# A float64 weight conversion in four planned stages, and stores of transformed rows issued from ScalarE's queue

## The chip, the cores and the metric

The kernel runs on one core of one Trainium2 chip. The metric is the device time of one execution in microseconds (us). The core has a matrix engine (TensorE, PE in the profile; its weight loads are PEld), a vector engine (VectorE, DVE), a scalar engine (ScalarE, ACT), a general engine (GpSimd, POOL) and an engine that here only issues DMA transfers (SyncE, SP). Each engine works through its own instructions in order. SP, ACT and POOL can issue transfers; "SPq" and "ACTq" in the profile are their issuing queues, and a transfer that has to wait there holds back whatever the same engine issues or computes behind it.

## The reference

```python
def reference(x, w_r, w_i, b_r, b_i, moe_w_in, moe_w_out, moe2_w_gate, moe2_w1, moe2_w2, moe2_capacity):
    X = np.fft.rfft(x, axis=1)                       # x: 8 x 3072 x 256
    Yr = X.real @ w_r - X.imag @ w_i + b_r
    Yi = X.real @ w_i + X.imag @ w_r + b_i
    Yr, Yi = (np.sign(v) * np.maximum(np.abs(v) - 0.01, 0) for v in (Yr, Yi))
    y = np.fft.irfft(Yr + 1j * Yi, n=3072, axis=1).astype(np.float32)
    x = y.reshape(8 * 3072, 256)
    h = x @ moe_w_in                                 # float64 weights, 256 x 2048
    g = np.where(h > 0, h, np.exp(np.minimum(h, 0)) - 1)
    x = (g @ moe_w_out).astype(np.float32)           # float64 weights, 2048 x 256
    # top-1 routing to 8 experts with a capacity: gate, pack, two matmuls
    # (256 -> 1024 -> 256, relu between), scaled by the gate and put back
    return moe2(x, moe2_w_gate, moe2_w1, moe2_w2, moe2_capacity)
```

## The kernel before

**The stages.** The 3072-point transforms are done in two steps of 96 and 32 points as matmuls. The first transform has steps s1 (line 144, its result `zo` stored to DRAM as `zs`) and s2 (line 174, reads `zi` back); then comes the spectral product `mix` (L219 to L237; `k` is a copy of one matmul's result, L221, which the matmul of L224 waits for); then the inverse transform with i1 (L249, result copied to `vo` and stored as `vs` by ACT, L253 and L254) and i2 (L273, reads `vi` back from `vs`, ACT copies the result to `yt`, L274, and SP stores it as `ys`, L276). The rows in `ys` are the tokens of the feed-forward part: `load_y` (L434) reads them as `y`, `split_y` (L442, L443) splits them into two parts `x`, `up` (L456 to L464) and `down` (L478) are its two matmuls. The experts follow (L582 and on). Only the first 14 chunks of 512 tokens, from a little over two batches, are worked out unconditionally; that is all that this profile holds.

**The float64 weights.** `moe_w_in` and `moe_w_out` come as float64. They are converted in 16 pieces of 128 by 512 numbers, 8 of each (`f64_piece`, L410; `f64_parts`, L376 to L397), into two float32 parts that are kept in SBUF: `win` and `wout`. A piece is a load `fv` of 512 KB by SP, a Square on ACT (`fsq`, L388), six VectorE instructions (L389, L390, L391, L393, L395, L396), a cast on ACT (L392, the first part) and two POOL instructions (L394, L397, the second part). All of its tiles, `fv`, `fsq`, `fh`, `fa` and `fb`, have a single buffer, so that a piece can only be loaded once the one before has been read.

**What sets the order.** The front of the program, up to the first matmuls of the feed-forward part, is a `plan`: a list of (time, piece of work), sorted by time and run by `run_until(t)`. One unit of time is one step `u` of `smi_pieces` (s2, and mix a little later); a batch has `nu` = 12 of them. The 16 weight pieces are spread over the times 1 to 28 with the whole piece at one time. A scheduler then orders each engine's instructions, with the plan's order as its priority, except that transfers issued through `load` (L114) keep the program's order on SP. The constants of the routing part (`wg`, `id`, `fv`<-`cst`, `e`, `tok`, and the cast of L821 that reads that `fv`) are loaded between `run_until(2 * nu + 3)` and `run_until(2 * nu + 6)`, thus ahead of the last weight piece.

Of the kernel before, what the change touches and what calls it, by code (L numbers as in the profile page):

```python
# [13 lines left out]
I32 = mybir.dt.int32  # L14
AF = mybir.ActivationFunctionType
ALU = mybir.AluOpType
# [15 lines left out]
MIX_LAG, I1_LAG = 2.2, 4.15  # L32
S1_AHEAD, X_AHEAD = 3, 2
S1_END, I2_END = 4, 4
W_SPAN = 1, 28
W_EARLY = 4
FF_START, FF_STEP = -1.8, 0.5

# [78 lines left out]
def f32(ap):  # L117
    return ap.bitcast(F32)


class Fft:
# [142 lines left out]
    def i2(self, i, ys, m=NA):  # L264
        nc = self.nc
        v = self.vt.pop(i)
        g, dh, h = i // 4, i // 2 % 2, i % 2
        if h == 0:
            self.yt = self.p["y"].tile([128, NA, 8], F32, name="yt")
        ps = self.bank("i2", [128, 512])  # L270
        pv = ps[:, 0:4 * m].rearrange("p (j n) -> p j n", j=4)
        for j in range(4):
            nc.tensor.matmul(pv[:, j, :], v[:, j, :], self.k["f2"][:, 0:m])  # L273
        nc.scalar.copy(self.yt[:, 0:m, 4 * h:4 * h + 4].rearrange("p n j -> p j n"), pv)  # L274
        if h == 1:
            nc.sync.dma_start(ys[dh, :, g, 0:m, :], self.yt[:, 0:m, :])  # L276


def fft_consts(tc, pool, tmp, cst, w_r, w_i, b_r, b_i):
# [95 lines left out]
def f64_parts(tc, tmp, src, p1, p2):  # L375

    nc, n = tc.nc, int(np.prod(src.shape[1:]))
    v = tmp.tile([128, 2 * n], I32, name="fv").rearrange("p (n t) -> p n t", t=2)
    sv = src.bitcast(I32)
    load(tc, v, sv.rearrange("p (n t) -> p n t", t=2) if len(sv.shape) == 2  # L380
                      else sv.rearrange("p a (n t) -> p a n t", t=2))
    hi, lo = v[:, :, 1], v[:, :, 0]
    sq = tmp.tile([128, n], F32, name="fsq")
    h = tmp.tile([128, n], I32, name="fh")
    a = tmp.tile([128, n], I32, name="fa")
    b = tmp.tile([128, n], I32, name="fb")
    least = float(np.array([0x380C0000], np.uint32).view(np.float32)[0])
    nc.scalar.activation(sq, f32(hi), AF.Square)  # L388
    nc.vector.scalar_tensor_tensor(f32(h), sq, least * least, f32(hi), op0=ALU.is_ge, op1=ALU.mult)  # L389
    nc.vector.tensor_scalar(a, h, 3, 0x3FFFFFF8, op0=ALU.logical_shift_left, op1=ALU.bitwise_and)  # L390
    nc.vector.scalar_tensor_tensor(b, h, -0x40000000, a, op0=ALU.bitwise_and, op1=ALU.bitwise_or)  # L391
    nc.scalar.copy(p1, f32(b))  # L392
    nc.vector.tensor_scalar(a, b, -0x00800000, None, op0=ALU.bitwise_and)  # L393
    nc.gpsimd.tensor_tensor(f32(b), f32(b), f32(p1), op=ALU.subtract)  # L394
    nc.vector.tensor_scalar(h, lo, 1, None, op0=ALU.logical_shift_right)  # L395
    nc.vector.scalar_tensor_tensor(sq, h, 2.0 ** -51, f32(a), op0=ALU.mult, op1=ALU.mult)  # L396
    nc.gpsimd.tensor_tensor(p2, f32(b), sq, op=ALU.add)  # L397


def scatter(tc, group, dst, idx, src, rows, free=True):  # L400
# [8 lines left out]
def f64_piece(tc, tmp, w_in, w_out, win, wout, i):  # L409

    if i < 8:
        a, c = divmod(i, 4)
        sl = slice(c * 512, c * 512 + 512)
        f64_parts(tc, tmp, w_in[a * 128:a * 128 + 128, sl], *(w[:, a, sl] for w in win))
    else:
        fs = slice(2 * (i - 8), 2 * (i - 8) + 2)
        f64_parts(tc, tmp, w_out.rearrange("(f p) d -> p f d", p=128)[:, fs, :],
                  *(w[i - 8].rearrange("p f d -> p (f d)") for w in wout))


# [281 lines left out]
def kernel(ctx, tc, x, w_r, w_i, b_r, b_i, moe_w_in, moe_w_out, w_gate, w1, w2, cst, out, cap):  # L702
    nc = tc.nc
# [13 lines left out]
    ys = [dr1.tile([2, 128, 4, NA, 8], F32, name=f"ys{b}") for b in range(3)]  # L717
# [7 lines left out]
    win = [wpool.tile([128, 2, DFF], F32R, name=f"win{i}") for i in (1, 2)]  # L725
    wout = [[], []]
# [19 lines left out]
    fp.update({n: mk(s1st, "f_" + n, b, side="right") for n, b in dict(x=3, z=2).items()})  # L746
    fp0["z"] = Cycle(fp["z"], mk(x0st, "f_z0", 2))

    def w_piece(i):
        f64_piece(tc, fp["f64"], moe_w_in, moe_w_out, win, wout, i)  # L750

    k, kfirst = fft_consts(tc, fp["c"], fp["sh"], cst, w_r, w_i, b_r, b_i)
    tags = dict(s1=["pd"], s2=["pb", "pc"], mix=["pa"], i1=["pd"], i2=["pd"])
# [20 lines left out]
    def i2p(b, m=NA):  # L774
        return [lambda i=i: i2(b, i, m) for i in range(-1, 16)]
# [4 lines left out]
    def at(t0, t1, pieces):  # L780
        plan.extend((t0 + (t1 - t0) * (n + 0.5) / len(pieces), len(plan) + n, f) for n, f in enumerate(pieces))

    def run_until(t):
        plan.sort(key=lambda v: v[:2])
        while plan and plan[0][0] < t:
            plan.pop(0)[2]()
# [19 lines left out]
    at(0.5, nu - S1_END, s1p(1)[S1_AHEAD:])  # L806
    at(nu - 1, 2 * nu - S1_END, s1p(2))
    at(2 * nu - S1_END, 2 * nu - S1_END, [free_s1])
    at(nu - 0.8 + I1_LAG, 2 * nu + I2_END, i2p(0))
    at(*W_SPAN, [lambda i=i: w_piece(i) for i in range(16)])  # L810
    at(-0.4, -0.4, [lambda: fs[0].load_z(0), lambda: fs[0].load_z(1)])
    run_until(2 * nu + 3)

    rt["wg"] = rtp.tile([128, E, D], F32, name="wg")
    load(tc, rt["wg"], w_gate.rearrange("(o e) d -> o e d", o=1).to_broadcast([128, E, D]))
# [16 lines left out]
    nc.vector.memset(row0[:, D + 1:D + 2].bitcast(I32), OOB)  # L832
    zero = row0[:, 0:D]
    row0b = row0.rearrange("p (o w) -> p o w", o=1)
    run_until(2 * nu + 6)
    rest = [i2p(1), i2p(2, 32)]
    tabv = tab.rearrange("(t p) w -> p t w", p=128)
    f64st.close()
# [9 lines left out]
    def src(c):  # L848
        return ys[c // 6], (c % 6) * 16

    run_until(2 * nu + nu // 2 - 0.9 + I1_LAG)
    moe.load_y(0, *src(0))
    for dh in range(2):
        moe.split_y(0, dh)
    agst.close()
# [96 lines left out]
def tail(tc, mk, rt, data, scratch, weights, tab, cap, slots, n_static):  # L952
# [4 lines left out]
    with ExitStack() as ph:  # L957
# [13 lines left out]
        with tc.If(load() > 0):  # L971
            with ExitStack() as pw:
# [3 lines left out]
                with ExitStack() as p0:  # L976
                    tmp = mk(p0, "t_f64", 1)
                    for i in range(16):
                        f64_piece(tc, tmp, *weights, win, wout, i)
                with tc.For_i(b0, B, 1) as b:  # L980
                    with tc.If(load() > 0):
                        with ExitStack() as p1:
# [63 lines left out]
```

## Time and profile before

| quantity | value |
|---|---|
| median of 3 runs | 1246.75 us (1244.53 to 1247.54) |
| the profiled execution | 1245.34 us |
| its span | 1243.4 us |
| mean granted TensorE clock | 0.979 |
| busy: PE, DVE, ACT, POOL | 1186.8, 802.7, 729.5, 305.7 us |

The span is the stretch from the first to the last instruction of the profiled execution; its time is 1.9 us longer. Busy time counts what an engine computes; the granted clock is the share of its full 2.4 GHz at which TensorE was let run.

### The profile page before, as it was taken

How to read it: one execution, taken by the hardware profiler on the slowest of the kernel's cores; microseconds unless marked ns; L12 is line 12 of the kernel's file. 1: busy time of each engine (PE TensorE's matmuls, PEld its weight loads, DVE VectorE, ACT ScalarE, POOL GpSimd, SP SyncE). 2: the span in 40 equal slices, each digit the busy share in tenths (PEclk: the TensorE clock that was granted, in tenths of full speed). 3: DMA queues.
4: the chain of work that ended last, by engine and by line, in shares of the span. 5: the costliest groups of instructions: out<-in, count | busy, mean ns of one | idle time of the engine just before them, and what ended most of it. 6: DMA issues, size and time to landing. Idle time of an engine off the chain costs nothing.

```text
span 1243.4 us, 21292 instructions
## 1 busy us (share of the span) xinstructions
PE 1186.8 (95%) x7862; PEld 1074.3 (86%) x7862; DVE 802.7 (65%) x2032; ACT 729.5 (59%) x1413; POOL 305.7 (25%) x395
## 2 busy tenths in 40 slices
PE   7899999899999999999999999999998999999994
PEld 2677789789999889999998899999997999999994
DVE  0688566543968768678588798788788644355430
ACT  4566666566676666666667566666665544445430
POOL 1244223311131231321213312313224211111111
PEclk9899899899999999999999999999998999999997
DMA  9986678545120211333424223312102622232100
GB/s 267 302 260 215 200 217 261 156 130 172 49 67 26 73 52 32 126 101 103 136 88 142 69 70 117 103 51 83 61 5 82 214 95 99 100 111 99 48 22 28
DMA packets 122834, 144.07 MB, mean 116 GB/s; under 512 B 7986, under 2 KB 106147, under 8 KB 122592
## 3 DMA queue, kind: packets, MB, share of 16 engines
q1 hardware_dynamic: 72688, 78.01, 20.5%
q10 hardware_dynamic: 45040, 51.96, 12.5%
q0 software_dynamic: 4992, 12.64, 2.9%
q8 instruction: 64, 1.05, 0.4%
q14 instruction: 50, 0.41, 0.1%
HBM read 72.23 MB, written 71.41 MB: 116 GB/s over the span
## 4 chain that ended last, share of the span: by engine, by line
PE 67%; DVE 12%; ACT 6%; DMA 6%; issue 6%; POOL 1%; SPq 0%; ACTq 0%; POOLq 0%; DVEq 0%
PE pm L478 21%; PE pa L456 21%; PE eup L649 9%; PE edown L662 8%; DVE lw L503 4%; DMA fv<-in_moe_w_out 3%; DVE e L462 2%; PE fi L273 2%; PE fmix L230 2%; PE fs L144 2%; ACT yt L274 1%; DMA zs<-zo 1%; DVE g L464 1%; ACT e L461 1%; PE fs L174 1%
## 5 line engine op out<-in xcount | busy, mean ns | idle before, releaser
L478 PEld LDWEIGHTS pm<-wout,g 128*128 128x128 f32 x2688 | 352.4, 191 | 19.3 <-DVE g L464 0.7
L478 PE MATMUL pm<-wout,g 128*128 128x256 f32 x2688 | 358.0, 283 | 0.5 <-DVE g L464 0.5
L456 PE MATMUL pa<-x,win 128*128 128x512 f32 x1344 | 353.1, 398 | 0.9 <-DVE e L462 0.9
L456 PEld LDWEIGHTS pa<-x,win 128*128 128x128 f32 x1344 | 239.1, 190 | 41.8 <-DVE e L462 1.8
L463 ACT CAST g<-e 128x512 fp32r<-128x512 f32 x224 | 138.7, 620 | 160.4 <-DVE e L462 159.8
L503 DVE SCALAR_TENSOR_TENSOR lw<-row,wg 128x256 bf16<-128x256 f32 x432 | 214.1, 496 | 12.1 <-ACT row L484 4.3
L462 DVE SCALAR_TENSOR_TENSOR e<-pa,e 128x512 f32<-128x512 f32 x224 | 153.4, 687 | 89.8 <-ACT e L461 88.9
L464 DVE TENSOR_TENSOR g<-e,g 128x512 fp32r<-128x512 f32 x182 | 145.9, 803 | 57.6 <-ACT g L463 53.9
L460 ACT ACTIVATE e<-pa 128x512 f32<-128x512 f32 x224 | 134.2, 599 | 50.0 <-PE pa L456 48.1
L461 ACT ACTIVATE e<-e 128x512 f32<-128x512 f32 x224 | 141.2, 633 | 5.1
L649 PE MATMUL eup<-ex,ew 128*128 128x384 f32 x768 | 142.8, 343 | 0.9 <-ACT ex L631 0.6
L662 PE MATMUL edown<-ew,eh 128*128 128x256 f32 x1152 | 140.8, 281 | 0.0
L464 POOL TENSOR_TENSOR g<-e,g 128x512 fp32r<-128x512 f32 x42 | 54.6, 1300 | 346.9 <-ACT g L463 309.1
L649 PEld LDWEIGHTS eup<-ex,ew 128*128 128x128 f32 x768 | 134.9, 191 | 2.8 <-DVE eh L651 1.2
L662 PEld LDWEIGHTS edown<-ew,eh 128*128 128x128 f32 x1152 | 137.1, 188 | 0.2
L651 DVE SCALAR_TENSOR_TENSOR eh<-eup,eh 128x384 fp32r<-128x384 f32 x128 | 70.3, 555 | 51.3 <-ACT eh L650 51.3
L402 POOL DMA_INDIRECT out<-eo,er x48 | 46.7, 972 | 216.1 <-ACT ex L631 135.0
L650 ACT ACTIVATE eh<-eup 128x384 fp32r<-128x384 f32 x128 | 63.1, 493 | 53.5 <-PE eup L649 53.3
L610 DVE TENSOR_TENSOR ew<-ewraw,ew 128x512 fp32r<-128x512 f32 x64 | 42.1, 686 | 64.6 <-ACT ew L609 64.0
L665 ACT ACTIVATE eo<-edown,er 128x256 f32<-128x256 f32 x48 | 22.8, 475 | 90.6 <-PE edown L662 63.4
L402 POOL DMA_INDIRECT tab<-row,sl x56 | 59.3, 1059 | 56.1 <-DVE sl L554 43.3
L144 PE MATMUL fs<-xp,f 96*96 96x512 f32 x96 | 49.8, 651 | 10.0 <-DMA xp<-in_x 5.3
(128 smaller groups left out, 1244.7 us busy)
## 6 DMA issues: line engine op xcount, KB each, us to landing
out<-row ACTq DMA_DIRECT2D x48, 512.0 KB, 3.5
ewraw<-in_moe_w SPq DMA_DIRECT2D x29, 512.0 KB, 4.0
xp<-in_x SPq DMA_DIRECT2D x24, 384.0 KB, 5.2
zs<-zo ACTq DMA_DIRECT2D x24, 384.0 KB, 4.0
zi<-zs SPq DMA_DIRECT2D x36, 256.0 KB, 4.8
vs<-vo ACTq DMA_DIRECT2D x36, 256.0 KB, 2.6
vi<-vs SPq DMA_DIRECT2D x48, 192.0 KB, 3.5
y<-ys SPq DMA_DIRECT2D x28, 256.0 KB, 3.2
```

The source lines that it names most:

```text
L144: nc.tensor.matmul(ps[:NA].rearrange("p n d -> p (n d)"), self.k["f1"], x[:, h:h + 2, :].rearrange("p n d -> p (n d)"))
L402: i = tc.nc.gpsimd.indirect_dma_start(dst, bass.IndirectOffsetOnAxis(idx, 0), src, None, bounds_check=rows - 1, oob_is_err=False)
L456: nc.tensor.matmul(ps, l, r, start=n == 0, stop=n == len(ops) - 1)
L460: nc.scalar.activation(e, ps, AF.Exp)
L461: nc.scalar.activation(e, e, AF.Relu, bias=1.0, scale=-1.0)
L462: nc.vector.scalar_tensor_tensor(e, ps, 0.0, e, op0=ALU.max, op1=ALU.subtract)
L463: nc.scalar.copy(g1, e)
L464: (nc.gpsimd if f % 4 == 3 and f < NF - 1 else nc.vector).tensor_tensor(g2, e, f32(g1), op=ALU.subtract)
L478: nc.tensor.matmul(self.pm[c][h][:, o, :], l[:, ts], r[f // 2][:, f % 2, :], start=f == 0 and o == 0 and n == 0, stop=f == NF - 1 and o == ...
L503: v.scalar_tensor_tensor(T("lw", [128, D], BF16), row[:, t, 0:D], 1.0, rt["wg"][:, e, :], op0=ALU.mult, op1=ALU.mult, accum_out=pl[:, t, e ...
L649: nc.tensor.matmul(ps, l, r, start=i == 0, stop=i == len(ops) - 1)
L662: nc.tensor.matmul(ps, l[:, f, ts], r[:, f, :], start=f == 0 and i == 0, stop=f == NFE - 1 and i == 2)
```

## The change

A piece of the float64 conversion becomes a generator of four stages, and the plan runs each stage at its own time: the load at t, the Square 1.35 units later, the first four VectorE instructions at 1.5, the rest at 1.85; t of piece i is 1 + 27 i / 16. The shift of the low half (L395 of before) moves ahead of the instructions of its stage and writes into `fsq`, and the last VectorE instruction writes into `fh` in place of `fsq`. The store of `ys` is issued by ACT and not by SP. The i2 steps of batch 0 start half a unit later. The constants of the routing part are loaded after all 16 weight pieces, and the first `load_y` is called 1.1 units earlier. (The conditional rest of the program only runs the generator to its end.)

```diff
+W_STAGES = 0, 1.35, 1.5, 1.85
...
         if h == 1:
-            nc.sync.dma_start(ys[dh, :, g, 0:m, :], self.yt[:, 0:m, :])
+            nc.scalar.dma_start(ys[dh, :, g, 0:m, :], self.yt[:, 0:m, :])
...
     load(tc, v, sv.rearrange("p (n t) -> p n t", t=2) if len(sv.shape) == 2
                       else sv.rearrange("p a (n t) -> p a n t", t=2))
+    yield
     hi, lo = v[:, :, 1], v[:, :, 0]
...
     nc.scalar.activation(sq, f32(hi), AF.Square)
+    yield
     nc.vector.scalar_tensor_tensor(f32(h), sq, least * least, f32(hi), op0=ALU.is_ge, op1=ALU.mult)
+    low = sq.bitcast(I32)
+    nc.vector.tensor_scalar(low, lo, 1, None, op0=ALU.logical_shift_right)
     nc.vector.tensor_scalar(a, h, 3, 0x3FFFFFF8, op0=ALU.logical_shift_left, op1=ALU.bitwise_and)
     nc.vector.scalar_tensor_tensor(b, h, -0x40000000, a, op0=ALU.bitwise_and, op1=ALU.bitwise_or)
+    yield
     nc.scalar.copy(p1, f32(b))
     nc.vector.tensor_scalar(a, b, -0x00800000, None, op0=ALU.bitwise_and)
     nc.gpsimd.tensor_tensor(f32(b), f32(b), f32(p1), op=ALU.subtract)
-    nc.vector.tensor_scalar(h, lo, 1, None, op0=ALU.logical_shift_right)
-    nc.vector.scalar_tensor_tensor(sq, h, 2.0 ** -51, f32(a), op0=ALU.mult, op1=ALU.mult)
-    nc.gpsimd.tensor_tensor(p2, f32(b), sq, op=ALU.add)
+    nc.vector.scalar_tensor_tensor(f32(h), low, 2.0 ** -51, f32(a), op0=ALU.mult, op1=ALU.mult)
+    nc.gpsimd.tensor_tensor(p2, f32(b), f32(h), op=ALU.add)
...
-    def w_piece(i):
-        f64_piece(tc, fp["f64"], moe_w_in, moe_w_out, win, wout, i)
+    parts = []
+
+    def w_load():
+        parts.append(f64_piece(tc, fp["f64"], moe_w_in, moe_w_out, win, wout, len(parts)))
+        next(parts[-1])
...
-    at(nu - 0.8 + I1_LAG, 2 * nu + I2_END, i2p(0))
-    at(*W_SPAN, [lambda i=i: w_piece(i) for i in range(16)])
+    at(nu - 0.3 + I1_LAG, 2 * nu + I2_END, i2p(0))
+
+    for i in range(16):
+        t = W_SPAN[0] + (W_SPAN[1] - W_SPAN[0]) * i / 16
+        for d in W_STAGES:
+            at(t + d, t + d, [w_load if d == W_STAGES[0] else lambda i=i: next(parts[i], None)])
     at(-0.4, -0.4, [lambda: fs[0].load_z(0), lambda: fs[0].load_z(1)])
-    run_until(2 * nu + 3)
+    run_until(2 * nu + 6)
...
-    run_until(2 * nu + 6)
     rest = [i2p(1), i2p(2, 32)]
...
+    run_until(2 * nu + nu // 2 - 2 + I1_LAG)
+    moe.load_y(0, *src(0))
     run_until(2 * nu + nu // 2 - 0.9 + I1_LAG)
-    moe.load_y(0, *src(0))
     for dh in range(2):
         moe.split_y(0, dh)
```

Three places of the resulting order follow. Rows of the changed kernel carry its own line numbers: from L115 on they are one higher than before in the transform, and L392, L394, L395, L396, L399, L401 are the six VectorE instructions of a piece in their new order.

On SP, around the first loads of `vi` (the rows that i2 of batch 0 reads), before:

```order
L114 DMA fv<-in_moe_w_out 128x2x512
L114 DMA vi<-vs_73 96x4x128 x2
L114 DMA zi<-zs_71 128x2x256
L114 DMA xp<-in_x 96x1024
L114 DMA vi<-vs_73 96x4x128
L114 DMA zi<-zs_71 128x2x256
L114 DMA fv<-in_moe_w_out 128x2x512
L114 DMA xp<-in_x 96x1024
L114 DMA vi<-vs_73 96x4x128
L276 DMA ys_67<-yt 128x768
L114 DMA vi<-vs_73 96x4x128
```

and now:

```order
L115 DMA fv<-in_moe_w_out 128x2x512
L115 DMA xp<-in_x 96x1024
L115 DMA zi<-zs_71 128x2x256 x2
L115 DMA xp<-in_x 96x1024
L115 DMA fv<-in_moe_w_out 128x2x512
L115 DMA vi<-vs_73 96x4x128 x3
L115 DMA zi<-zs_71 128x2x256
L115 DMA xp<-in_x 96x1024
L115 DMA vi<-vs_73 96x4x128
L115 DMA fv<-in_moe_w_out 128x2x512
```

The stores of `ys` have left SP, two `zi`, two `xp` and one more `fv` stand ahead of the first `vi`, and an `fv` load stands directly ahead of it.

On VectorE, one piece of `moe_w_in` early in batch 0, before:

```order
L389 SCALAR_TENSOR_TENSOR fh<-fsq,fv 128x512
L390 TENSOR_SCALAR fa<-fh 128x512
L391 SCALAR_TENSOR_TENSOR fb<-fh,fa 128x512
L393 TENSOR_SCALAR fa<-fb 128x512
L395 TENSOR_SCALAR fh<-fv 128x512
L396 SCALAR_TENSOR_TENSOR fsq<-fh,fa 128x512
L198 TENSOR_TENSOR sm<-fs_689,im 128x256
```

and now two pieces, a little later in the batch, where one ends as the next begins:

```order
L399 TENSOR_SCALAR fa<-fb 128x512
L199 TENSOR_TENSOR sm<-fs_833,im 128x256
L200 TENSOR_TENSOR xr_839<-fs_833,xr_838 128x512
L235 TENSOR_TENSOR tt<-fmix,k_857 128x512
L199 TENSOR_TENSOR sm<-fs_883,im 128x256
L200 TENSOR_TENSOR xr_889<-fs_883,xr_888 128x512
L238 SCALAR_TENSOR_TENSOR tc<-tt,kb 128x512
L401 SCALAR_TENSOR_TENSOR fh<-fsq,fa 128x512
L235 TENSOR_TENSOR tt<-fmix,k_928 128x512
L392 SCALAR_TENSOR_TENSOR fh<-fsq,fv 128x512
L394 TENSOR_SCALAR fsq<-fv 128x512
```

The reader of `fv` (L394 now, L395 before) has moved from fifth to second place in a piece, and the last instruction (L401 now, L396 before) has moved behind six instructions of the transform here, to two places ahead of the next piece's first, which writes the same `fh`.

On ScalarE, near the end of the front, where the last weight piece's cast (`wout`) and the first token splits (`x`) stood, before:

```order
L392 CAST wout_1786<-fb 128x512
L236 ACTIVATE kb<-tt,lam 128x512
L187 COPY im<-fs_2477 128x256
L253 COPY vo<-fi_2494 128x512
L200 CAST xs_2484<-sm 128x256
L254 DMA vs_75<-vo 128x2x256
L253 COPY vo<-fi_2495 128x512
L221 COPY k_2517<-fmix 128x256
L254 DMA vs_75<-vo 128x2x256
L442 CAST x<-y 128x512
L236 ACTIVATE kb<-tt,lam 128x512
```

and now:

```order
L237 ACTIVATE kb<-tt,lam 128x512
L201 CAST xs_2465<-sm 128x256
L254 COPY vo<-fi_2475 128x512
L254 COPY vo<-fi_2476 128x512
L255 DMA vs_75<-vo 128x2x256 x2
L222 COPY k_2498<-fmix 128x256
L237 ACTIVATE kb<-tt,lam 128x512
L187 CAST xr_2553<-fs_2548 128x512
L188 COPY im<-fs_2548 128x256
L222 COPY k_2572<-fmix 128x256
L447 CAST x<-y 128x512
```

No weight cast is left here, and the first `x` comes four rows later, behind the next copy `k`.

## Rows read from the trace of the kernel before

**Rows 1.** Stretch, length, busy PE, PEld, DVE, ACT, POOL (instructions), granted clock, DMA share, GB/s.

```profile
40.00:130.00 90.00, 85.00 (x559) 66.78 (x557) 77.07 (x128) 60.08 (x133) 40.37 (x38) 0.98 0.77 241
130.00:141.00 11.00, 9.20 (x39) 6.99 (x40) 2.61 (x5) 4.41 (x10) 1.45 (x2) 0.69 1.01 269
141.00:186.00 45.00, 41.95 (x311) 36.94 (x310) 27.91 (x47) 29.37 (x59) 13.07 (x12) 0.97 0.68 209
218.00:232.00 14.00, 9.86 (x68) 8.61 (x67) 8.97 (x14) 6.99 (x16) 6.86 (x7) 0.88 0.33 105
232.00:242.00 10.00, 7.98 (x52) 7.52 (x53) 4.94 (x8) 6.60 (x15) 4.45 (x5) 0.83 0.61 189
262.00:1243.00 981.00, 954.66 (x6395) 890.22 (x6393) 645.41 (x1766) 573.27 (x1091) 220.63 (x298) 0.99 0.26 86
```

**Rows 2.** Timeline of TensorE: four of its stops (start, duration, idle before).

```profile
89.29 0.50 PE L224 MATMUL fmix<-bias,row 128*128 128x512 f32 x1 [1.58 <-ACT k L221]
...
131.80 1.94 PE L273 MATMUL fi<-f,vi 96*128 96x96 f32 x8 [1.88 <-DMA vi<-vs]
...
224.35 0.79 PE L224 MATMUL fmix<-bias,row 128*128 128x512 f32 x1 [3.55 <-ACT k L221]
...
237.53 0.69 PE L224 MATMUL fmix<-bias,row 128*128 128x512 f32 x1 [2.02 <-ACT k L221]
```

**Rows 3.** Waits from 40 to 245 us: total us, times, longest.

```profile
DVE fh L389 <- ACT fsq L388: 19.0, 9, 5.5
...
ACT fsq L388 <- DMA fv<-in_moe_w_out: 11.3, 7, 4.0
...
ACT win L392 <- DVE fb L391: 6.6, 6, 1.5
```

**Rows 4.** L396 over the whole run (ns minimum, median, maximum).

```profile
L396 DVE SCALAR_TENSOR_TENSOR fsq<-fh,fa x16: 693/1648/1792, 52.6 to 220.4; 128x512 f32<-128x512 int32 x16
```

**Rows 5.** Timelines of VectorE and of POOL at 89 us: one piece's L396 and L394.

```profile
89.14 1.79 DVE L396 SCALAR_TENSOR_TENSOR fsq<-fh,fa 128x512 f32<-128x512 int32 x1
...
89.09 1.29 POOL L394 TENSOR_TENSOR fb<-fb,win 128x512 f32<-128x512 f32 x1 [1.38 <-ACT win L392]
```

**Rows 6.** SP's own queue waits from 40 to 245 us.

```profile
SPq L114 <- DVE fh L395: 37.7, 10, 7.4
SPq L276 <- ACT yt L274: 25.5, 5, 8.9
SPq L276 <- ACT k L221: 23.1, 3, 9.6
SPq L114 <- DMA vs<-vo: 11.0, 1, 11.0
```

**Rows 7.** Timeline of SP, issues of 153, 210 and 223 us.

```profile
153.23 0.36 SPq L276 DMA_DIRECT2D ys<-yt  x1
153.68 0.42 SPq L114 DMA_DIRECT2D fv<-in_moe_w_out  x1
...
210.45 0.38 SPq L114 DMA_DIRECT2D fv<-in_moe_w_out  x1
...
223.75 1.30 SPq L434 DMA_DIRECT2D y<-ys  x2
```

**Rows 8.** Transfers issued from 40 to 245 us: count, KB each, median us to landing.

```profile
fv<-in_moe_w_out SPq DMA_DIRECT2D x8, 512.0 KB, 5.2
```

**Rows 9.** Timeline of ScalarE near the end of the front.

```profile
215.32 0.68 ACT L388 ACTIVATE fsq<-fv 128x512 f32<-128x512 f32 x1 [2.01 <-DMA fv<-in_moe_w_out]
...
222.97 0.41 ACT L200 CAST xs<-sm 128x256 fp32r<-128x256 f32 x1 [1.82 <-DVE sm L198]
222.98 0.37 ACTq L254 DMA_DIRECT2D vs<-vo  x1
...
227.62 0.62 ACT L442 CAST x<-y 128x512 fp32r<-128x512 f32 x1 [3.32 <-DMA y<-ys]
...
237.10 0.37 ACT L221 COPY k<-fmix 128x256 f32<-128x256 f32 x1 [0.47 <-ACT vo L253]
```

More of the change, by code (lines that the diff above doesn't have):

```diff
@@ L413, in f64_piece @@
         sl = slice(c * 512, c * 512 + 512)
-        f64_parts(tc, tmp, w_in[a * 128:a * 128 + 128, sl], *(w[:, a, sl] for w in win))
+        return f64_parts(tc, tmp, w_in[a * 128:a * 128 + 128, sl], *(w[:, a, sl] for w in win))
     else:
         fs = slice(2 * (i - 8), 2 * (i - 8) + 2)
-        f64_parts(tc, tmp, w_out.rearrange("(f p) d -> p f d", p=128)[:, fs, :],
+        return f64_parts(tc, tmp, w_out.rearrange("(f p) d -> p f d", p=128)[:, fs, :],
                   *(w[i - 8].rearrange("p f d -> p (f d)") for w in wout))
@@ L978, in tail @@
                     for i in range(16):
-                        f64_piece(tc, tmp, *weights, win, wout, i)
+                        for _ in f64_piece(tc, tmp, *weights, win, wout, i):
+                            pass
                 with tc.For_i(b0, B, 1) as b:
```

## Prediction

> **What bounds the kernel now.** I read the windows of busy time first, cut where TensorE's share changes, then TensorE's stops in the timeline, then the table of waits and SP's own queue. From 262 us to the end TensorE is busy for 954.66 of 981 us at a clock of 0.99 [rows 1], and the change leaves its order of instructions there as it was. So the feed-forward part and the experts take as long as before, and what the front (40 to 245 us) gains or loses reaches the end one for one. In the front a stretch loses its idle time, and busy time times (1 − granted clock), since a stop is followed by matmuls at the lower of TensorE's two clock levels. By [rows 1]: 40 to 130 us loses 5.0 idle + 0.02 × 85.0 = 6.7 us; 130 to 141 loses 1.8 + 0.31 × 9.2 = 4.65; 141 to 186 loses 3.05 + 0.03 × 41.95 = 4.3; 218 to 232 loses 4.14 + 0.12 × 9.86 = 5.3; 232 to 242 loses 2.02 + 0.17 × 7.98 = 3.4. That is 24.4 us, 2% of the whole, and the most that a change of the front's order can give.
>
> The reader is to see who releases TensorE. It is a copy on ScalarE in three of the four stops shown, and the return of `vi` in the fourth [rows 2]. ScalarE is not full (60.08 of 90 us from 40 to 130): it stands in line behind a weight piece. It waits for VectorE's `fb` before it can cast `win` (6.6 us in 6 waits) and for the load `fv` before it can square (11.3 us in 7) [rows 3], and `k`, `vo` and `xs` queue behind it. VectorE, the other link, is busy for 77.07 of those 90 us [rows 1].
>
> **The conversion in stages: 40 to 130 us.** The instructions stay the same in number and size; only places and buffers change. The pieces follow each other by (220.4 − 52.6)/15 = 11.2 us [rows 4] for 27/16 = 1.69 units, 6.6 us a unit. The load now leads its Square by 1.35 units, 8.9 us, where it lands in 5.2 [rows 8]; but it can only be issued once the piece before has given `fv` back, which its second VectorE instruction does at 0.19 units before, so 1.16 units or 7.7 us remain: enough. The cast stands 0.35 units, 2.3 us, behind the stage that makes `fb`, so the 6.6 us of waits for `fb` should mostly go. L396 takes 693 ns alone and 1648 in the median [rows 4]; in [rows 5] it starts 0.05 us after POOL's L394 and lasts until 0.55 us after its end. In the new order no shift stands between the mask instruction and its successor L401, and in places L401 stands six instructions later, so that it should often miss POOL's subtraction. That would be up to 0.96 us a piece, some 8 us over the eight or nine pieces of this stretch. These two sources (6.6 and 8) exceed the 6.7 us that TensorE loses, but they overlap, and the nine pieces stay on an engine that is 86% busy. I take two thirds, **−4.5 us** (bounds: 0, when the waits only move, and −6.7).
>
> The Trainium skill gives a reason for the long L396 in "SBUF — State Buffer", section "Who interferes with whom": VectorE's second port pair is GpSimd's only one, under an exclusive lock that goes to whichever issues first. The trace agrees: 1.79 us beside a 1.29 us POOL instruction. By that rule the gain here hangs on which of the two starts first, and a piece where POOL starts first gains nothing.
>
> **The first `vi`: 130 to 141 us.** TensorE waits 1.88 us for `vi`, which waited 11.0 us on SP for the store of `vs` [rows 2, 6]. The store is as late as before, since ScalarE issues it after the last i1 of batch 0, and i2 that starts half a unit later in the plan has its first matmul at the same place among TensorE's instructions. But two `zi`, two `xp` and an `fv` now go ahead of the first `vi`. I take **0** (bounds: −4.65, all of it, and the delay priced as a rival below).
>
> **Batch 0's i2 under batch 1: 141 to 186 us.** On SP a load waited 37.7 us in 10 waits for L395 to release `fv`, and the `ys` stores 25.5 and 23.1 us for ScalarE's copies [rows 6]; SP is in order, so an `fv` load stood behind such a store, as at 153.23 and 153.68 us [rows 7], and ScalarE and then VectorE (19.0 us in 9 waits [rows 3]) waited for the piece. With the stores on ScalarE's own queue, right behind the copy that they need, and the load 1.35 units ahead, these waits should shrink to little. I take **−3** of 4.3 us (bounds 0 and −4.3).
>
> **The end of the front: 218 to 242 us.** The last weight piece was loaded at 210.45 us, behind the constants [rows 7]; its Square held ScalarE until 215.32 and its VectorE part made `xs` wait 1.82 us at 222.97 [rows 9], out of which comes TensorE's 3.55 us stop at 224.35 [rows 2]. Now all 16 pieces are over before the constants. **−4.5** of 5.3 us (bounds −2 and −5.3; the rest is the wait for `tc`, which no weight piece causes). Then ScalarE held `k` behind an `x` that waited 3.32 us for `y`, and behind `vo` [rows 9], and TensorE stopped for 2.02 us at 237.53. The `y` load was issued at 223.75 [rows 7], after the last `wout`; it is now called earlier, and the next `k` stands ahead of the first `x`. **−2.5** of 3.4 us (bounds 0 and −3.4).
>
> **What it costs.** Eight `ys` stores in the front go to ScalarE, at 0.36 us (SP's row [rows 7]) to 0.37 (ScalarE's [rows 9]) each: 3 us of ScalarE's time, of which I put half on the path, since ScalarE releases three of the four stops shown but not each store stands ahead of one: **+1.5** (bounds 0 and 3). The 16 others lie in the feed-forward part, where ScalarE has slack: from 262 us on it is busy for 573 of 981 us. New is also that the last VectorE instruction writes `fh`, which POOL's last addition reads, so that the next piece's first VectorE instruction waits for POOL; before, its Square waited for that. The nearest row is POOL's 1.29 us [rows 5]; where one piece ends just ahead of the next, as in the second order shown, some 0.7 us of it remain behind one transform instruction. For some three such places in the crowded stretch: **+2** (bounds 0 and 16 × 1.29 = 21, if every piece paid in full and all of it reached TensorE).
>
> **Sum.** −4.5 + 0 − 3 − 4.5 − 2.5 + 1.5 + 2 = −11. The profiled execution took 1245.34 us (span 1243.4), so it would take 1234.3; the median before is 1.4 us higher, so a median of about **1235.5 us**.
>
> **The rivals.** About 0.3%, 3.7 us, is what a measurement of this kernel can tell from no change.
>
> *Only the end of the front gains.* VectorE's work is not less, the collisions with POOL stay, and the waits behind a piece are only cut into smaller ones. For it: VectorE's 86%. Against: TensorE stops for ScalarE's place in line, not for VectorE alone. Then −4.5 − 2.5 + 3.5 = −3.5 us: 1243, at the edge of no change; with the end half as good, 1246. Chance 0.15.
>
> *The store's move gives nothing.* The fv load then still waits, for L394 in place of `yt`, and the −3 falls away: 1238.5. For it: most of SP's wait is for L395, 37.7 us, not for the copies of any one store. Chance 0.15. In "DMA: Bandwidth & Descriptors", section "Issuing engines are not separate DMA queues", the Trainium skill says that another issuing engine saves only the issuing time on the sequencer, which is small. The rows differ: SP stood 48.6 us behind `ys` stores, which is a wait in an in-order queue and no issuing time; by that rule the sum would be as in this rival.
>
> *SP is held by `fv` in front of `vi`: slower.* There is one `fv` buffer, and an `fv` load now stands directly ahead of `vi` loads at the first i2 and at five later pieces, asking earlier than before for a buffer that VectorE gives back no earlier. Such a wait was 3.8 us on average (37.7/10) and 7.4 at most [rows 6]. If `vi` has no slack, six such waits cost 22.6 us on TensorE, and 22.6 − 11 gives 1258. It decides from half of that on, 11.3 us. Against it: the reader of `fv` has moved from fifth to second place in a piece, and `vi` has three buffers. Chance 0.1.
>
> *All the losses go*, that of 130 to 141 us too, and POOL costs nothing: −24.4 + 1.5 = −23, 1224. Chance 0.1.
>
> **How the numbers follow.** The forecast, a gain of 5 to 16 us (1231 to 1242 on the median's scale), has 0.5. The range leaves out the slower rival and the better part of the largest gain, and takes in the bounds of the four gains: 1227 to 1246. Faster by over 0.3%: 0.5 + 0.15 + 0.1 and a little of the first rival, 0.77; the same 0.13; slower 0.10.
>
> **What would show it.** Right: ScalarE's waits for `fv` and for `fb` nearly gone; L401 with a median near 0.7 us; no stop at `k` of 3.55 us near 224; the first feed-forward matmuls some 11 us earlier, and the rest of the run equally long. Wrong: VectorE waiting for POOL's addition ahead of each piece; SP waiting on L394 with `vi` behind it, and TensorE on `vi` for more than 2 us more than once; L401 still at 1.6 us; or a stretch after 262 us that is longer than before, which would break the one-for-one rule on which the sum stands.

## The result, and the profile after

The changed kernel takes 1229.94 us (median of five executions, 1228.54 to 1235.73), against 1246.18 us before in the same comparison. The ratio, taken over all executions, is 0.989, with a 95% interval of 0.986 to 0.992: some 14 us faster. The forecast was 1235.5 us, in a range of 1227 to 1246, and faster; it holds. Three of the five executions took 1228.5 to 1229.9 us at a mean granted clock of 0.985 to 0.987, and two took 1235.5 and 1235.7 us at 0.979, so a difference of a few us between single executions can be one of the clock. The profiled execution is one of the first kind, 1229.94 us, with a span of 1228.0 us and a mean granted clock of 0.985.

The windows of the kernel after, at the same times as [rows 1] (the last one to the end of its shorter span):

```profile
40.00:130.00 90.00, 80.76 (x549) 64.85 (x549) 76.28 (x131) 62.84 (x135) 41.46 (x40) 1.00 0.84 256
130.00:141.00 11.00, 11.00 (x69) 9.08 (x70) 3.73 (x6) 5.63 (x11) 3.62 (x3) 0.84 0.95 272
141.00:186.00 45.00, 42.98 (x332) 38.15 (x330) 29.72 (x54) 31.36 (x62) 15.16 (x14) 1.00 0.74 233
218.00:232.00 14.00, 11.15 (x91) 9.70 (x89) 5.96 (x10) 8.01 (x19) 6.89 (x6) 1.00 0.57 170
232.00:242.00 10.00, 10.00 (x63) 9.22 (x64) 6.07 (x11) 6.28 (x14) 2.20 (x3) 0.83 0.55 164
262.00:1228.00 966.00, 942.30 (x6329) 880.19 (x6327) 639.73 (x1759) 566.91 (x1079) 219.70 (x297) 0.99 0.26 86
```

From 40 to 130 us TensorE is busy for *less* than before (80.76 against 85.00 us), at a clock of 1.00 instead of 0.98, so the idle time there has not gone: it is 9.2 us instead of 5.0. The stretches from 218 to 242 us are better filled, 21.15 us busy of 24 against 17.84. But fixed times do not tell where a gain arose once the two programs are apart. For that, the same instruction is looked up in both: the first, the fifteenth and the thirty-third matmul of the bias (L224 before, L225 after), and the last count of the routing part (`pk`). In the timeline of TensorE before:

```profile
46.19 0.40 PE L224 MATMUL fmix<-bias,row 128*128 128x512 f32 x1
...
128.10 0.40 PE L224 MATMUL fmix<-bias,row 128*128 128x512 f32 x1
...
247.82 0.40 PE L224 MATMUL fmix<-bias,row 128*128 128x512 f32 x1
...
957.92 0.19 PE L541 MATMUL pk<-oh,u 128*128 128x32 bf16 x1
```

and after:

```profile
42.93 0.40 PE L225 MATMUL fmix<-bias,row 128*128 128x512 f32 x1
...
124.66 0.40 PE L225 MATMUL fmix<-bias,row 128*128 128x512 f32 x1
...
238.62 0.39 PE L225 MATMUL fmix<-bias,row 128*128 128x512 f32 x1
...
941.59 0.19 PE L546 MATMUL pk<-oh,u 128*128 128x32 bf16 x1
```

The differences give the time of each stretch:

| stretch | before | after | change |
|---|---|---|---|
| start to the first (the first weight load is issued at 39 to 41 us) | 46.19 | 42.93 | −3.3 |
| first to second: batch 0, most of the `moe_w_in` pieces | 81.91 | 81.73 | −0.2 |
| second to third: the other pieces, the end of the front | 119.72 | 113.96 | −5.8 |
| third to fourth: feed-forward part | 710.10 | 702.97 | −7.1 |
| fourth to the end: experts | 285.48 | 286.41 | +0.9 |

So of 15.4 us between the two spans, 3.3 arise at the start, where SP issues the same transfers in the same order up to the first weight load (the fourteen profiles of this study have this first row between 42.93 and 46.19 us), some 6 in the front, and 7 in the feed-forward part, which the prediction held to be unchanged.

TensorE's stops of over a microsecond in the front after, the counterparts of [rows 2]:

```profile
57.40 1.13 PE L175 MATMUL fs<-ag,zi 128*128 128x128 f32 x8 [1.56 <-DVE tc L238]
75.46 1.10 PE L145 MATMUL fs<-xp,f 96*96 96x512 f32 x2 [1.19 <-ACT vo L254]
88.86 0.50 PE L225 MATMUL fmix<-bias,row 128*128 128x512 f32 x1 [1.35 <-ACT k L222]
...
129.85 1.32 PE L274 MATMUL fi<-f,vi 96*128 96x96 f32 x8 [3.38 <-DMA vi<-vs]
...
187.24 2.46 PE L250 MATMUL fi<-tc,ag 64*128 64x256 f32 x14 [2.69 <-ACT yt L275]
...
231.96 1.13 PE L250 MATMUL fi<-tc,ag 64*128 64x256 f32 x8 [2.45 <-DVE tc L238]
```

The stops of 3.55 us at 224 and 2.02 us at 237 are gone; the one at `vi` is still there. The one of 2.69 us at `yt` stands where the kernel before had two, of 0.69 us at 151 and of 1.89 us here:

```profile
181.21 1.13 PE L273 MATMUL fi<-f,vi 96*128 96x96 f32 x8 [1.89 <-ACT yt L274]
```

The waits from 40 to 232 us, for [rows 3] and for `yt`:

```profile
DVE fh L392 <- ACT fsq L390: 5.9, 5, 2.1
ACT yt L275 <- DMA ys<-yt: 5.1, 3, 3.4
ACT fsq L390 <- DMA fv<-in_moe_w_out: 5.0, 4, 2.0
...
ACT win L398 <- DVE fb L396: 4.3, 5, 1.3
```

SP's own queue in the same stretch, for [rows 6]:

```profile
SPq L115 <- PE fi L274: 37.4, 11, 7.9
SPq L115 <- DVE fsq L394: 34.6, 10, 6.7
```

And the last VectorE instruction of a piece, for [rows 4]:

```profile
L401 DVE SCALAR_TENSOR_TENSOR fh<-fsq,fa x16: 691/693/1809, 51.5 to 204.1; 128x512 f32<-128x512 int32 x16
```

Its median fell from 1648 to 693 ns, as forecast. The waits around a piece are shorter, and the 48.6 us that SP stood at `ys` stores are gone; SP now waits for TensorE to give a `vi` buffer back, thus because it is ahead, while its wait for the `fv` buffer is much as before (34.6 us against 37.7). ScalarE's wait for the store of the one `yt` buffer to land has grown from 1.3 to 5.1 us.

The short instruction does not in the main come from missing POOL. In fifteen of the sixteen pieces of before, POOL's subtraction L394 starts 0.04 to 0.86 us ahead of L396, which then takes 0.97 to 1.79 us. In eight pieces of the changed kernel the two still overlap, but L401 starts first and takes 0.69 to 0.70 us, and POOL's subtraction behind it takes 1.36 to 1.71 us where it took some 1.3. One such pair:

```profile
61.51 0.69 DVE L401 SCALAR_TENSOR_TENSOR fh<-fsq,fa 128x512 f32<-128x512 int32 x1
61.64 1.71 POOL L400 TENSOR_TENSOR fb<-fb,win 128x512 f32<-128x512 f32 x1 [3.66 <-DVE fa L399]
```

### The profile page after: what moved, and what is told of

Its sections match the earlier page's. It is cut to its first block, busy times and chain, and to the rows that moved or that the text cites. A ratio compares the mean times of both kernels' runs of the same rounds, so it can differ in the third digit from the quotient of the medians.

```text
span 1228.0 us, 21274 instructions
## 1 busy us (share of the span) xinstructions
PE 1177.9 (96%) x7862; PEld 1068.3 (87%) x7862; DVE 796.2 (65%) x2032; ACT 732.5 (60%) x1413; POOL 306.2 (25%) x395
## 4 chain that ended last, share of the span: by engine, by line
PE 74%; DMA 8%; DVE 7%; issue 5%; ACT 3%; POOL 1%; SPq 0%; ACTq 0%; POOLq 0%; DVEq 0%
PE pa L461 23%; PE pm L483 23%; PE eup L654 9%; PE edown L667 8%; DVE lw L508 3%; PE fi L274 3%; PE fs L145 2%; PE fmix L231 2%; PE fi L250 1%; PE fmix L220 1%; DVE e L467 1%; DMA fv<-in_moe_w_in 1%; DMA zs<-zo 1%; PE fs L175 1%; POOL out L407 1%
```

## The experiments

All were compared with the kernel before on the same chip; its median was 1245.7 to 1247.6 us in these comparisons, so the ratios are what can be set against each other. The stretches in the table are between the same four instructions as above, each of one profiled execution. Four profiles of kernels whose front is ordered exactly as before (before, e6, e9, e10) give 118.8 to 122.3 us for the second stretch, so there only differences of several us mean something; the feed-forward stretch repeats better, 708.5 to 710.2 us in the six of before, e2, e3, e4, e5 and e7.

| kernel | ratio to before (95%) | median us | 46–128 | 128–248 | feed-forward |
|---|---|---|---|---|---|
| before | 1 | 1246.18 | 81.9 | 119.7 | 710.1 |
| changed | 0.989 (0.986 to 0.992) | 1229.94 | 81.7 | 114.0 | 703.0 |
| e1 store alone | 0.991 (0.990 to 0.993) | 1235.63 | 82.4 | 118.3 | 703.7 |
| e2 stages and constants alone | 0.996 (0.995 to 0.998) | 1243.13 | 81.3 | 120.0 | 710.0 |
| e3 constants alone | 1.0015 (1.0005 to 1.0025) | 1248.46 | 82.6 | 119.2 | 708.8 |
| e4 changed, store back on SP | 0.995 (0.993 to 0.997) | 1239.70 | 81.0 | 117.7 | 708.7 |
| e5 store of batch 0 alone | 0.997 (0.995 to 0.998) | 1241.77 | 82.5 | 116.9 | 710.2 |
| e6 store of batches 1, 2 alone | 0.993 (0.991 to 0.996) | 1237.39 | 82.4 | 118.8 | 702.6 |
| e7 order inside a piece alone | 0.9988 (0.9972 to 1.0003) | 1244.22 | 83.9 | 119.0 | 708.5 |
| e8 changed, times back | 0.995 (0.994 to 0.997) | 1240.06 | 80.8 | 116.5 | 703.2 |
| e9 expert weights off SP | 1.003 (1.001 to 1.004) | 1249.83 | 82.7 | 121.7 | 712.6 |
| e10 expert weights earlier | 0.997 (0.995 to 0.999) | 1243.06 | 81.9 | 122.3 | 705.8 |
| e11 changed, pieces whole | 0.987 (0.985 to 0.990) | 1230.50 | 81.4 | 109.5 | 703.6 |
| e12 store and times alone | 0.991 (0.989 to 0.993) | 1236.21 | 82.2 | 119.1 | 702.6 |

**The store alone.**

```diff
-            nc.sync.dma_start(ys[dh, :, g, 0:m, :], self.yt[:, 0:m, :])
+            nc.scalar.dma_start(ys[dh, :, g, 0:m, :], self.yt[:, 0:m, :])
```

> The kernel before with one part of the change: the ys store issued by ScalarE. Theory A (the store holds SP, and the loads of fv and vi stand behind it): SP's waits at the ys stores (48.6 us) disappear, ScalarE's waits for fv (11.3 us) shrink, and the time falls by 2 to 4 us, to about 1243. Rival B (another issuing engine saves its issuing time alone): within 1.5 us of before, since SP's loads then wait for the fv buffer instead.

It is 11 us faster, outside of what either theory gave. The feed-forward stretch is 6.4 us shorter; in the front one profile tells little. SP's waits at the `ys` stores are gone, but its waits for L395 to give `fv` back grew from 37.7 to 53.8 us, as rival B said, and ScalarE's waits for `fv` did not shrink: 11.3 us for `moe_w_out`, as before. So theory A has the right edit, and neither the place nor the way in which it pays.

**The stages alone.** The changed kernel with these three edits taken back:

```diff
-            nc.scalar.dma_start(ys[dh, :, g, 0:m, :], self.yt[:, 0:m, :])
+            nc.sync.dma_start(ys[dh, :, g, 0:m, :], self.yt[:, 0:m, :])
...
-    at(nu - 0.3 + I1_LAG, 2 * nu + I2_END, i2p(0))
+    at(nu - 0.8 + I1_LAG, 2 * nu + I2_END, i2p(0))
...
-    run_until(2 * nu + nu // 2 - 2 + I1_LAG)
-    moe.load_y(0, *src(0))
     run_until(2 * nu + nu // 2 - 0.9 + I1_LAG)
+    moe.load_y(0, *src(0))
```

> The kernel before with the four stages, the new order inside a piece and the constants behind all 16 pieces; the ys store stays on SP, i2 and load_y stay at their old times. Theory A (stages and constants carry the gain at the end of the front, the store and the y load the rest): 1238 to 1241. Rival B (the stages are the whole change): as the changed kernel, 1230 to 1234. Rival C (the stages without the store's move leave fv behind the ys stores, and the lead is lost): 1243 or more.

Rival C by its number (1243.13 us, at its edge), though still 4.6 us faster by the ratio: SP stands 33.5 and 21.6 us at the `ys` stores, as before, and the feed-forward part is as before.

**The constants alone.**

```diff
-    run_until(2 * nu + 3)
+    run_until(2 * nu + 6)
...
-    run_until(2 * nu + 6)
     rest = [i2p(1), i2p(2, 32)]
```

> The kernel before with the constants' loads behind all 16 pieces, and nothing else; each piece stays whole. Theory A (the last piece is late because the constants stand ahead of it): the 3.55 us stop near 224 us shrinks or goes, the time falls by 3 to 5 us, to 1241 to 1243. Rival B (the piece as a whole lump is what holds ScalarE, wherever it stands): the stop moves to another place, time 1245 to 1247.

Rival B, with a time a little above its number: 0.15% longer. TensorE's order of instructions is that of before, and its 3.55 us stop at `k` has moved to an earlier matmul, at 2.74 us:

```profile
215.74 0.80 PE L224 MATMUL fmix<-bias,row 128*128 128x512 f32 x1 [2.74 <-ACT k L221]
```

**The store back on SP**, all else changed (the first edit of e2 alone):

> The changed kernel with the ys store back on SP. Theory A (the store's move is worth the 3 us of the sum): 1233 to 1236, and SP waits at ys stores while fv and vi stand behind. Rival B (the move is worth nothing): 1229 to 1232, as the changed kernel.

It was slower than either: 0.995, so that the store is worth some 7 us in the changed kernel, and its feed-forward stretch is 708.7 us, as before.

**The store by batch.**

```diff
-            nc.sync.dma_start(ys[dh, :, g, 0:m, :], self.yt[:, 0:m, :])
+            (nc.scalar if self.b == 0 else nc.sync).dma_start(ys[dh, :, g, 0:m, :], self.yt[:, 0:m, :])
```

and with `self.b > 0` in the other (`b` is the number of the batch).

> The kernel before with the ys stores of batch 0 alone (8, all in the front) issued by ScalarE; the 16 later ones stay on SP. Theory A (the gain of the store's move lies behind the front, where the loads of y and vi stood behind it on SP): 0 to 3 us faster, and from 270 us to the end as long as before, some 970 us of the profiled span. Rival B (the front is where it pays): 6 to 11 us faster.

> The kernel before with the ys stores of batches 1 and 2 alone (16, all beside the feed-forward part) issued by ScalarE. Theory A: 5 to 8 us faster, the front as before and the stretch from 270 us to the end 5 to 6 us shorter (some 964 us), at the chunk boundaries near 450 and 690 us. Rival B: within 2 us of before.

Neither forecast fits fully: the eight stores of batch 0 give 4 us (0.997), between theory A's 0 to 3 and rival B's 6 to 11, and the sixteen later ones 8 to 9. Only the later ones shorten the feed-forward part, by 7.5 us. In e6 TensorE's instructions stand in exactly the order of before; what differs is the order on VectorE, ScalarE and POOL behind the front. What the stores of batch 0 gain by is not shown: in e5 too SP's wait for the `fv` buffer grew, to 53.7 us, and ScalarE waited 7.9 us for `fv`.

**The order inside a piece.** The kernel before with the new order and buffers, and nothing else.

```diff
+    low = sq.bitcast(I32)
+    nc.vector.tensor_scalar(low, lo, 1, None, op0=ALU.logical_shift_right)
     nc.vector.tensor_scalar(a, h, 3, 0x3FFFFFF8, op0=ALU.logical_shift_left, op1=ALU.bitwise_and)
...
-    nc.vector.tensor_scalar(h, lo, 1, None, op0=ALU.logical_shift_right)
-    nc.vector.scalar_tensor_tensor(sq, h, 2.0 ** -51, f32(a), op0=ALU.mult, op1=ALU.mult)
-    nc.gpsimd.tensor_tensor(p2, f32(b), sq, op=ALU.add)
+    nc.vector.scalar_tensor_tensor(f32(h), low, 2.0 ** -51, f32(a), op0=ALU.mult, op1=ALU.mult)
+    nc.gpsimd.tensor_tensor(p2, f32(b), f32(h), op=ALU.add)
```

> The kernel before with the new order inside a weight piece alone (the shift second, the last VectorE instruction into fh); each piece stays whole and at its old time. Theory A (a long last VectorE instruction beside POOL's subtraction is not what TensorE waits for): within 2 us of before, whether or not its median falls from 1.65 us. Rival B, the prediction's term for 40 to 130 us: 3 to 5 us faster.

This is theory A, and the cleanest of the runs. The last VectorE instruction is as short as in the changed kernel:

```profile
L397 DVE SCALAR_TENSOR_TENSOR fh<-fsq,fa x16: 683/693/1797, 53.1 to 221.3; 128x512 f32<-128x512 int32 x16
```

The time is that of before (0.999, 0.997 to 1.000), and the stretch in which this was to give 4.5 us took 83.9 us, against 81.9. TensorE's order is that of before here, too.

**The two times back.** The last two edits of e2.

> The changed kernel with i2 of batch 0 and the first load_y at their old times; stages, store and constants stay changed. Theory A (the two shifted times are worth the 2.5 us that the prediction put on the first y): 2 to 3 us slower than the changed kernel, about 1233. Rival B (they are worth nothing): 1229 to 1231. Rival C (without the later start of i2, i2 and the weight pieces collide on ScalarE): 4 us or more slower.

Rival C: some 8 us less gain than the changed kernel, in executions from 1233.7 to 1243.7 us. TensorE has a stop at `vo` that the changed kernel has not:

```profile
137.06 1.96 PE L145 MATMUL fs<-xp,f 96*96 96x512 f32 x2 [3.51 <-ACT vo L254]
```

The profiled execution, 1233.7 us, is the fastest of twelve, so its stretches understate what the times are worth. That the stop arises from a collision of i2 with the weight pieces, as rival C has it, is not shown by this run alone; e12 below bears on it.

**What in the feed-forward part.** In all profiles so far whose later stores are on SP, TensorE stops at the chunk boundary near 690 us; in the others it does not. VectorE is full ahead of it: it works on the 32 instructions of the routing part (L503), and at this one chunk also on the first expert weights (L610). Two kernels move only these, with the stores left on SP. Loads of the first expert weights from ScalarE's queue:

```diff
-        eng = self.nc.scalar if 4 <= q < 7 else self.nc.sync
+        eng = self.nc.scalar if q < 7 else self.nc.sync
```

> The kernel before with the first four loads of expert weights issued by ScalarE's queue in place of SP's, so that no ys store stands ahead of them; the ys stores stay on SP. In the resulting order 7 of the 8 first conversions of expert weights on VectorE (L610) lie inside the routing block (32 instructions of L503) ahead of the chunk boundary near 690 us; before it is 5, and 2 with the later stores on ScalarE. Theory A (these conversions inside the full block make TensorE stop at the boundary): no gain there, rather 1 to 3 us slower than before. Rival B (the load that waits on SP is itself what costs): 3 to 5 us faster, and the stop near 690 us is gone.

And the conversion called sooner:

```diff
-        if sp0 and g % 4 == 3:
+        if sp0 and g % 2 == 1:
```

> The kernel before with the four pieces of the first expert's weight conversion called at every second step of the feed-forward loop in place of every fourth; the ys stores stay on SP. 1 of the 8 conversions is left inside the routing block. Theory A: the stop near 690 us is gone and the stretch behind it 3 to 5 us shorter, as with the stores on ScalarE, about 1241 to 1243. Rival B (SP's queue matters, not the order): within 1.5 us of before.

Theory A in both. The windows of VectorE's L610 from the start of the routing block to its end, and of 10 us behind it (length, busy time with the number of L610, granted clock, DMA share, GB/s), before:

```profile
665.00:697.00 32.00, 2.74 (x4) 1.00 0.21 67
700.00:710.00 10.00, 0.00 (x0) 0.91 0.32 107
```

with the later stores on ScalarE (e6):

```profile
659.00:690.00 31.00, 1.37 (x2) 1.00 0.22 71
690.00:700.00 10.00, 0.00 (x0) 1.00 0.27 92
```

with the expert weights off SP (e9):

```profile
666.80:700.00 33.20, 5.20 (x6) 1.00 0.25 80
700.00:710.00 10.00, 0.00 (x0) 0.66 0.20 66
```

and with them earlier (e10):

```profile
665.90:697.00 31.10, 0.69 (x1) 1.00 0.25 82
697.00:707.00 10.00, 0.00 (x0) 1.00 0.34 114
```

Four, two, six and one conversions lie in the block by the trace (the counts of 5 and 7 given ahead of the runs are one too high). From the first `pk` of the boundary before to that of the boundary behind (649.7 to 745.0 us before) the four kernels take 95.3, 91.0, 98.0 and 91.0 us, and the changed one 91.0. So with up to two nothing is lost, four cost 4.3 us here and six cost 7.0. The other profiles agree: those with the later stores on SP and the conversion as before (before, e2, e3, e4, e5, e7) have four conversions in the block and take 47.5 us up to the stop's `pk` (649.7 to 697.1 before), and those with them on ScalarE (changed, e1, e6, e8, e11, e12) have two and take 45.3. (In e4 and e7 the clock behind the stop stayed at 1.00, and four cost 3.1 us in all.) The stop itself, in the kernel before:

```profile
683.10 1.45 PE L478 MATMUL pm<-wout,g 128*128 128x256 f32 x10 [0.48 <-DVE g L464]
697.12 0.19 PE L541 MATMUL pk<-oh,u 128*128 128x32 bf16 x1 [1.13 <-DVE oh L521]
697.96 0.18 PE L541 MATMUL pk<-bf,u 128*128 128x32 bf16 x1 [0.65 <-POOL bf L529]
```

and in e9, where it is one of 3.25 us:

```profile
700.07 0.21 PE L541 MATMUL pk<-oh,u 128*128 128x32 bf16 x1 [3.25 <-DVE oh L521]
```

The rest of the cost is the lower clock in the 10 us behind it. (In e9 four of TensorE's matmuls at this boundary also stand in another order than before; in e10 TensorE's order is that of before.)

**Whole pieces in the changed kernel.**

```diff
-        for d in W_STAGES:
-            at(t + d, t + d, [w_load if d == W_STAGES[0] else lambda i=i: next(parts[i], None)])
+        at(t + W_STAGES[1], t + W_STAGES[1], [lambda i=i: (w_load(), list(parts[i]))])
```

> The changed kernel with each weight piece whole again, at its Square's time (1.35 units behind t), in the new inner order; store, constants and the two shifted times stay changed. Theory A (the stages give little, the store and the times give the rest): 1230 to 1235. Rival B (the load ahead and the spread carry the front's gain): 1236 to 1240, with ScalarE waiting for fv again, 8 us or more in all.

Theory A: the stages can be undone at no cost (0.987, from four executions, against 0.989, with intervals that overlap).

**Store and times, with no edit of the conversion.** The kernel before with the edit of e1 and the two times of the change.

> The kernel before with the ys store on ScalarE and the two shifted times (i2 of batch 0 half a unit later, the first load_y 1.1 units earlier), and no edit of the weight conversion at all: pieces, their times and the constants stay as before. Theory A (the conversion's edits and the constants' place are worth little; what the run with whole pieces showed comes from store and times): 1229 to 1234. Rival B (the last piece behind the constants still costs its stop, so store and times alone are not enough): 1235 to 1239, with TensorE's stop at k near 220 us still there.

Rival B by its number: 1236.21 us, as the store alone, and some 5 us behind e11 (the intervals of the two just touch, but each of the six executions of e12 is slower than each of the four of e11). So what lies between e12 and e11, the piece's new order, its time half a unit later and the constants behind the last piece, is worth those 5 us together, while the constants alone (e3) and the order alone (e7) give nothing.

Rival B's reason is not borne out. Near 220 us TensorE's stops at `k` are of 0.75 and 0.78 us only. The second stretch is 9.6 us longer than in e11, and 5.9 us of it lie between the fifteenth and the seventeenth matmul of the bias, from 126 to 147 us and far ahead of the last piece, where e12 has the stop at `vo` that e8 has:

```profile
138.47 2.02 PE L144 MATMUL fs<-xp,f 96*96 96x512 f32 x2 [3.62 <-ACT vo L253]
```

e11 and the changed kernel have no such stop there. In the plan the changed kernel, e2, e4, e8 and e11 have the Square of a piece half a unit later than before (1.35 units behind t against 0.84), and the changed kernel, e4, e11 and e12 have i2 half a unit later. So three of the fourteen kernels move only one of the two, and these have a stop of over a microsecond at `vo` between 126 and 152 us: e2 (3.27 us), e8 (3.51) and e12 (3.62). The others have none there but one of 0.57 us (e4). This fits a collision of i2 with the pieces, as rival C of e8 has it, but no run moves i2 alone.

## Why the prediction was right, and where it was not

The time fell by 14 us where 11 were forecast, but the sum came out by terms that were not all there: the 11 were to come from the front, and there the profiles give some 6, beside 3.3 at the start, which the edits do not touch. That the gain of the feed-forward part, forecast as nothing, fills the place of what the front did not give is luck. The signs named in advance came in part: the stop near 224 us is gone and L401 is at 0.7 us, but ScalarE's waits for `fv` and `fb` fell only from 11.3 to 5.0 and from 6.6 to 4.3 us, and what lies behind 262 us did not stay as long as before, so that the one-for-one rule of the sum does not hold.

- **"The feed-forward part and the experts take as long as before"** is the step that failed. It took only TensorE's order to be unchanged, which it was, and overlooked that the order of VectorE and ScalarE behind the front changes as well. The term is −7.1 us in the profiles. For 4.3 of it the mechanism is shown by e9 and e10: how many expert weight conversions lie inside a full VectorE block, which follows from the sixteen later stores (e6). The other 2.7 lie between 399 and 502 us. From 399 to 453 us of before, 1.3 go with the later stores as well: 52.0 to 52.6 us in the six kernels that have them on ScalarE, 53.5 to 53.9 in the eight others; by what wait is not shown. From 453 to 502 us, 1.4 are not the store's: there the profiles take 49.4 or 47.9 us as the clock behind a stop was low or not (last section), 49.5 in e1 with the stores on ScalarE and 47.9 in e3 with them on SP. Why the store's queue decides that order is open too: that these weight loads no longer stand behind a store on SP is not the reason by itself, since e9 gave them another queue and the conversions went later.
- **40 to 130 us, −4.5:** nothing (−0.2). The two sources were there, the cast's waits shrank and L401 is short, but what they save does not reach TensorE. e7 shows it for the last instruction, and e11 for the spread; in all fourteen profiles this stretch takes 80.8 to 83.9 us. The prediction set the time saved on VectorE and ScalarE against TensorE's loss, but showed no row that leads from the one to the other: TensorE's stop at 89.29 us, for `k` [rows 2], is still there with 1.35 us. The lead of the load was misread, too: the piece before gives `fv` back 0.19 units ahead of the load, so the whole 1.35 units remain and not 1.16; nothing in the sum hangs on it.
- **The first `vi`, 0:** near; the stop grew from 1.88 to 3.38 us. TensorE comes to it 3.45 us sooner, 3.3 of them by the start, and `vi` comes 1.95 us sooner.
- **141 to 186 us, −3, by the store:** e5 puts batch 0's stores at 4 us in the whole front, which is the size. The way there is not the forecast one: without the stages the loads of `fv` then wait for their buffer (53.8 us in e1) and ScalarE for `fv` as long as before (11.3 us). Not in the list of costs was ScalarE's wait for the single `yt` buffer, 5.1 us where it was 1.3; TensorE waits 2.69 us for `yt` at 187 us, no more than the 0.69 and 1.89 us of before.
- **The end of the front, −4.5 and −2.5:** the two stops went, and the wait for `tc` behind them grew from 0.59 to 2.45 us. That the last piece's place is worth 4.5 us is not shown: e3 shows that the constants alone only move the stop, and of the 9.6 us between the profiles of e11 and e12 5.9 arise by 147 us. The two shifted times are worth some 8 us in the changed kernel (e8) and nothing without the conversion's edits (e12 against e1), and the stop at `vo` near 138 us stands where only one of the two was moved (e8, e12). So these terms do not add up; the prediction added them.
- **The costs, +3.5:** eight stores on ScalarE still leave a gain of 4 us (e5), and VectorE's wait for POOL's addition is 1.5 us in three waits in the changed kernel, where the sum had 2.
- **The rival of the Trainium skill**, "DMA: Bandwidth & Descriptors", section "Issuing engines are not separate DMA queues", by which the store's move would save the issuing time alone, does not fit this kernel: e1 gave 11 us. The 24 stores of about 0.36 us would be 8.6 us of issuing on SP, but TensorE does not wait for SP's issuing: e10 shortens the stretch from 649.7 to 745.0 us by as much as e6, with every store left on SP. What was gained in that stretch is another order, of which the section does not speak. The lock in "SBUF — State Buffer", section "Who interferes with whom", agrees with the trace: 1648 ns in the median [rows 4] and 1.79 us in the piece shown [rows 5], where POOL's subtraction starts first, and 693 ns in the new place, where in eight of the sixteen pieces VectorE starts first and POOL's subtraction is the longer one. So in half of the pieces the wait was turned over to POOL and not avoided.

## What to carry to other kernels

When a scheduler sets the engines' orders, an edit far from a stretch can reorder it: compare the orders of all engines over the whole program, not only TensorE's, before a stretch is called unchanged. A crowded engine is not yet the limit: shortening its instructions by a microsecond each gave nothing where TensorE waited for something else. And cost a set of edits by undoing each and by doing each alone; here the four stages, named first in the title, could be taken out again for nothing, and the store's queue alone gives 11 of the 14 us.

## What the runs showed that was not expected

A stop of 3.25 us at 700 us was followed by 10 us at a granted clock of 0.66 (e9), and the two stops of 1.78 us together at 697 us of before by 10 us at 0.83:

```profile
697.00:707.00 10.00, 9.23 (x47) 7.96 (x48) 6.00 (x17) 5.85 (x10) 4.77 (x12) 0.83 0.24 79
```

At this boundary the clock stayed at 1.00 where TensorE had no stop, but in e4 and e7 also behind the two stops of before. With the lower clock such a stop cost about two times its length: 7.0 us in e9 against e6.

But the length of a stop does not settle what follows. At the chunk boundary near 450 us TensorE waits 2.1 to 2.3 us for `yt` in all fourteen profiles. Before, and in the changed kernel:

```profile
452.97 0.18 PE L541 MATMUL pk<-oh,u 128*128 128x32 bf16 x1 [2.31 <-ACT yt L274]
...
442.49 0.18 PE L546 MATMUL pk<-oh,u 128*128 128x32 bf16 x1 [2.30 <-ACT yt L275]
```

The 10 us behind this stop, in before, the changed kernel, e1 and e3:

```profile
453.00:463.00 10.00, 10.00 (x58) 8.91 (x58) 5.40 (x13) 7.20 (x13) 5.35 (x8) 0.84 0.50 153
...
442.50:452.50 10.00, 10.00 (x64) 8.99 (x64) 5.96 (x13) 7.40 (x13) 5.70 (x8) 1.00 0.26 94
...
449.20:459.20 10.00, 10.00 (x57) 9.11 (x57) 5.38 (x13) 7.23 (x13) 5.71 (x8) 0.83 0.26 94
...
452.40:462.40 10.00, 10.00 (x64) 9.00 (x64) 5.81 (x14) 7.31 (x14) 5.30 (x7) 1.00 0.46 140
```

The clock is 0.83 or 0.84 in nine of the profiles and 1.00 in the five others, and the stretch to the next boundary takes 49.4 us or 47.9. It goes neither with the store's queue nor with the share of the DMA. So 1.4 us between two single profiles can be the clock behind one stop, and are no gain of an edit; why it falls in one and not in the other is open.
